# Channel attention on one core: fewer rows read twice, by a smaller accumulator and a stash in PSUM

## Chip, cores, metric

The kernel runs on one core of one Trainium2 chip. The metric is the device time of one execution in microseconds; medians are quoted. Engine names are those of the profile: PE (matmul), DVE (VectorE), ACT (ScalarE), SP (SyncE, which here only issues loads). A "row" below is one pixel of 96 bf16 channels in each of the 128 partitions: 192 bytes per partition, 24.6 KB in all.

## The reference

```python
H = W = 384; C = 96; r = 24                 # x: (1, 384, 384, 96) bf16, w1: (96, 24), w2: (24, 96)
gap = jnp.mean(xf, 1); gmp = jnp.amax(xf, 1)  # over all 147456 pixels
h_a = relu(gap @ w1);  h_m = relu(gmp @ w1)
scale = sigmoid(h_a @ w2 + h_m @ w2)          # one factor per channel
return x * scale[:, None, None, :]
```

The output needs a factor that depends on all of x. So x is read once for the mean and the maximum, kept on the chip as far as it fits, and then multiplied and stored. Each partition has 1152 rows, 221,184 bytes, which is more than its part of the on-chip memory (SBUF) can hold beside the other tiles.

## The kernel before

Phase 1 loads x in chunks of 64 rows. DVE folds each chunk into `acc`, 64 rows of running maxima; PE adds the rows up with a column of ones. The cache holds NCR = 1028 rows; U = 124 rows don't fit. Those are loaded first, into places that later chunks overwrite, and must be read a second time in phase 2.

```python
ACC_ROWS = 64; FIRST_P2_CHUNKS = (16, 32); TAIL_P1_CHUNK = 16; LAG = 6; PA_SLOT = 1
...
    NCR = min(NPP, budget // ROWB)      # rows in the cache
    U = NPP - NCR                       # rows that are read twice
...
    # phase 1, for each chunk
        nc.sync.dma_start(out=xt, in_=xv[:, r0 : r0 + n, :])
        ...
                nc.vector.tensor_tensor(out=acc[:, 0:m, :], in0=acc[:, 0:m, :],
                                        in1=xt[:, a : a + m, :], op=ALU.max)
        ...
    # then a tree over the 64 rows of acc, transpose, two small matmuls, sigmoid -> scale
    # phase 2: rows of the U are loaded into acc (64 rows), srow (8 rows) and,
    # once its first contents are stored, a place in the cache (52 rows)
            nc.sync.dma_start(out=ap, in_=xv[:, r : r + n, :])
    ...
    for ci, (r0, n) in enumerate(chunks2):
        mult(ap, n)          # DVE: cache rows *= scale
        store(r0, n, ap)     # DMA issued by ACT
        ...
                nc.sync.dma_start(out=u["ap"], in_=xv[:, u["r0"] : u["r0"] + u["n"], :])
        while loaded and loaded[0][0] + LAG <= ci:
            _, u = loaded.pop(0)
            mult(u["ap"], u["n"])
            store(u["r0"], u["n"], u["ap"])
```

## Time and profile before

| | before |
|---|---|
| median time | 159.76 us (159.47 to 159.88) |
| span of the profile | 157.7 us |
| HBM read / written | 31.37 MB / 28.31 MB |
| phase 1, DMA rate 8 to 66 us | 426 GB/s |
| last DVE maximum done / column maxima (`pmax`) done / `scale` ready | 74.5 / 78.8 / 80.8 us |
| stores, DMA rate 100 to 140 us | 430 GB/s |

The two rows of the page below cut the span into 40 slices of 3.94 us: the busy share of the 16 DMA engines in tenths, and what they moved.

```profile
DMA  5999999999999999950179999999999999999995
GB/s 184 407 437 433 424 433 421 419 436 418 433 415 440 415 427 419 425 208 0 50 259 399 390 399 287 374 436 420 430 433 423 428 436 433 424 440 421 427 436 212
```

DMA is full in phase 1 and again in phase 2; between them, in slices 18 and 19 (the first is slice 0), it has little or nothing to do. From the last load packet of phase 1 (its end is at 70.7 us) to the first store (issued at 81.85 us) it is 11 us; this stretch is called the bubble below. (The Trainium skill, "HBM Reference", section "Specifications (TRN2)", says that a core streaming alone gets about 425 GB/s; this trace agrees with 426 and 430.)

The next view groups instructions by line and shape: busy time in all, mean ns of one, then the idle time in front of them and what ended it.

```profile
L169 DVE TENSOR_TENSOR acc<-acc,cache 128x6144 bf16<-128x6144 bf16 x14 | 47.0, 3358 | 6.6 <-DMA cache<-in_x_dram 6.6
L232 DVE TENSOR_TENSOR cache<-cache,scale 128x6144 bf16<-128x6144 bf16 x15 | 49.3, 3348 | 0.0
L192 DVE TENSOR_TENSOR acc<-acc 128x3072 bf16<-128x3072 bf16 x1 | 1.8, 1759 | 0.0
```

A 64-row maximum takes 3.36 us and its chunk comes every 3.69 us, so DVE waits for DMA. A 64-row multiply takes 3.35 us; the DMA needs 1.573 MB / 430 GB/s = 3.66 us to store it. DMA is the limit in both phases, and DVE is close behind.

The chain of waits (start us, us, what) around the bubble:

```profile
70.30 3.17 DVE acc L169
73.49 0.97 DVE acc L169
74.48 1.77 DVE acc L192
...
78.55 0.22 DVE pmax_sb L201
...
80.58 0.26 ACT scale L229
```

The last chunks' maxima are done at 74.46 us, and a tree of six steps, of which the first takes 1.77 us, ends at 78.77 us. Then come the small steps to `scale`.

Stretches of phase 2 (window, length, busy us of each engine, PE clock, busy share of DMA, GB/s):

```profile
core 0: us, PE busy (x) PEld busy (x) DVE busy (x) ACT busy (x) POOL busy (x), PEclk, DMA share, GB/s
94.00:100.00 6.00, 0.00 (x0) 0.00 (x0) 6.00 (x2) 0.00 (x0) 0.00 (x0) 0.50 1.00 291
100.00:140.00 40.00, 0.00 (x0) 0.00 (x0) 39.99 (x14) 0.00 (x0) 0.00 (x0) 0.50 1.01 430
88.00:157.00 69.00, 0.00 (x0) 0.00 (x0) 51.99 (x17) 0.00 (x0) 0.00 (x0) 0.50 0.99 409
```

One thing stands out: from 94 to 100 us the DMA engines are as busy as ever (share 1.00), but move 291 GB/s. The 52-row re-read into the cache was issued at 92.4 us.

### The profile page before, as it was taken

The numbers are of one execution on the slowest core, as the hardware profiler recorded it, in microseconds if no ns is written. First come the engines' busy times: TensorE is split into PE (matmuls) and PEld (weight loads), VectorE is DVE, ScalarE is ACT, GpSimd is POOL, SyncE is SP. The second block draws the span as 40 slices with busy tenths as digits, with TensorE's granted clock in tenths as the row PEclk, the third lists the DMA queues.
The fourth block names the chain that finished last, engine by engine and source line by source line (L and its number), as shares of the span: only waits on it lengthen the run. The fifth ranks groups of instructions, "written<-read, shape, count | busy, mean of one in ns | idle before, by whom it ended". The sixth has DMA issues, their size and how long they took to land.

```text
span 157.7 us, 798 instructions
## 1 busy us (share of the span) xinstructions
PE 54.6 (35%) x299; PEld 26.2 (17%) x299; DVE 122.9 (78%) x51; ACT 2.5 (2%) x6; POOL 0.7 (0%) x6
## 2 busy tenths in 40 slices
PE   0299777739977777688010000000000000000000
PEld 0144333314433333334000000000000000000000
DVE  0258999959999999899969999999999999950000
ACT  3000000000000000001010000000000000000000
POOL 1000000000000000000000000000000000000000
PEclk9999999996999999999655555555555555555555
DMA  5999999999999999950179999999999999999995
GB/s 184 407 437 433 424 433 421 419 436 418 433 415 440 415 427 419 425 208 0 50 259 399 390 399 287 374 436 420 430 433 423 428 436 433 424 440 421 427 436 212
DMA packets 6343, 59.72 MB, mean 379 GB/s; under 512 B 836, under 2 KB 1092, under 8 KB 1604
## 3 DMA queue, kind: packets, MB, share of 16 engines
q1 hardware_dynamic: 3168, 31.36, 48.8%
q10 hardware_dynamic: 3172, 28.32, 42.9%
q8 instruction: 2, 0.03, 0.1%
q14 instruction: 1, 0.01, 0.0%
HBM read 31.37 MB, written 28.31 MB: 379 GB/s over the span
## 4 chain that ended last, share of the span: by engine, by line
DMA 44%; DVE 39%; issue 2%; DVEq 2%; PE 1%; ACT 0%; SPq 0%
DMA cache<-in_x_dram 44%; DVE cache L232 31%; DVE acc L169 3%; DVE acc L192 3%; DVE acc L232 2%; DVEq L331 2%; DVE srow_full L232 0%; SPq L133 0%; PE pmaxT_full L206 0%; DVE vt L207 0%; DVE hp L222 0%; PE misc_ps L228 0%; ACT scale L229 0%; DVE pmax_sb L201 0%; PE misc_ps L220 0%
## 5 line engine op out<-in xcount | busy, mean ns | idle before, releaser
L169 DVE TENSOR_TENSOR acc<-acc,cache 128x6144 bf16<-128x6144 bf16 (+3 forms) x18 | 57.2, 3180 | 8.6 <-DMA cache<-in_x_dram 8.4
L179 PE MATMUL misc_ps<-cache,ones_col 128*1 128x384 bf16 x288 | 53.0, 342 | 20.5 <-DMA cache<-in_x_dram 20.5
L232 DVE TENSOR_TENSOR cache<-cache,scale 128x6144 bf16<-128x6144 bf16 (+4 forms) x19 | 55.6, 2991 | 0.6 <-ACT scale L229 0.6
L179 PEld LDWEIGHTS <-ones_col 128*1 128x1 bf16 x288 | 25.1, 87 | 48.0 <-issue 27.3
L150 DVE COPY acc<-cache 128x6144 bf16<-128x6144 bf16 x1 | 1.8, 1760 | 6.0 <-DMA cache<-in_x_dram 6.0
L192 DVE TENSOR_TENSOR acc<-acc 128x3072 bf16<-128x3072 bf16 (+4 forms) x5 | 3.9, 779 | 0.2
L232 DVE TENSOR_TENSOR acc<-acc,scale 128x6144 bf16<-128x6144 bf16 x1 | 3.3, 3348 | 0.0
L206 PE MATMUL pmaxT_full<-ident,pmax_sb 128*96 128x128 bf16 x1 | 0.3, 339 | 3.9 <-DVE pmax_sb L201 3.9
L209 ACT ACTIVATE srow_full<-misc_ps 1x384 f32<-1x384 f32 x1 | 0.5, 481 | 70.9 <-PE misc_ps L179 70.9
L95 ACT ACT_TABLE_LOAD x1 | 1.3, 1283 | 1.2 <-PEq L320 1.2
L211 PE MATMUL misc_ps<-one,srow_full 1*96 1x1 f32 x8 | 0.8, 221 | 0.6 <-ACT srow_full L209 0.6
L211 PEld LDWEIGHTS misc_ps<-one,srow_full 1*96 1x96 f32 x8 | 0.7, 159 | 1.0 <-ACT srow_full L209 1.0
L206 PEld LDWEIGHTS <-pmax_sb 128*96 128x96 bf16 x1 | 0.2, 155 | 4.0 <-DVE pmax_sb L201 4.0
L94 DVE MEMSET warm<- 128x1 f32 x1 | 0.1, 59 | 0.8 <-PEq L320 0.8
L222 DVE TENSOR_TENSOR hp<-hrelu 24x128 bf16<-24x128 bf16 x1 | 0.3, 281 | 0.5 <-ACT hrelu L221 0.5
L207 DVE TENSOR_REDUCE vt<-pmaxT_full 96x1 bf16<-96x128 bf16 x1 | 0.3, 290 | 0.4 <-PE pmaxT_full L206 0.4
L232 DVE TENSOR_TENSOR srow_full<-srow_full,scale 128x768 bf16<-128x768 bf16 x1 | 0.5, 549 | 0.0
L228 PE MATMUL misc_ps<-w_sb,hp 24*128 24x96 bf16 x1 | 0.3, 258 | 0.6 <-DVE hp L222 0.6
L220 PE MATMUL misc_ps<-vt,w_sb 96*24 96x2 bf16 x1 | 0.2, 181 | 0.4 <-DVE vt L207 0.4
masks.py:199 POOL TENSOR_SCALAR_AFFINE_SELECT ident<-ident 128x128 bf16<-128x128 bf16 x1 | 0.3, 294 | 0.1
L229 ACT ACTIVATE scale<-misc_ps 128x96 bf16<-128x96 f32 x1 | 0.3, 251 | 0.7 <-PE misc_ps L228 0.7
L221 ACT ACTIVATE hrelu<-misc_ps 24x2 bf16<-24x2 f32 x1 | 0.2, 161 | 4.6 <-PE misc_ps L220 4.6
(12 smaller groups left out, 1.5 us busy)
## 6 DMA issues: line engine op xcount, KB each, us to landing
cache<-in_x_dram SPq DMA_DIRECT2D x15, 1536.0 KB, 27.1
out_dram<-cache ACTq DMA_DIRECT2D x15, 1536.0 KB, 14.0
cache<-in_x_dram SPq DMA_DIRECT2D x2, 1440.0 KB, 19.0
acc<-in_x_dram SPq DMA_DIRECT2D x1, 1536.0 KB, 6.4
out_dram<-acc ACTq DMA_DIRECT2D x1, 1536.0 KB, 6.5
cache<-in_x_dram SPq DMA_DIRECT2D x1, 1344.0 KB, 29.1
cache<-in_x_dram SPq DMA_DIRECT2D x1, 1248.0 KB, 10.2
out_dram<-cache ACTq DMA_DIRECT2D x1, 1248.0 KB, 13.5
```

Source lines behind the costliest of these rows:

```text
L95: nc.scalar.activation(out=warm2[:], in_=warm[:], func=ACT.Sigmoid)
L150: nc.vector.tensor_copy(out=acc[:, 0:m, :], in_=xt[:, 0:m, :])
L169: nc.vector.tensor_tensor(out=acc[:, 0:m, :], in0=acc[:, 0:m, :], in1=xt[:, a : a + m, :], op=ALU.max,)
L179: nc.tensor.matmul(sum_ps[:, 0 : g * C], ones_col[:], xt[:, g0 : g0 + g, :], start=(mm_i == 0), stop=(mm_i == total_mm - 1),)
L192: nc.vector.tensor_tensor(out=acc[:, 0:h, :], in0=acc[:, 0:h, :], in1=acc[:, h : 2 * h, :], op=ALU.max)
L206: nc.tensor.transpose(pmaxT_ps, pmax_sb[:], ident[:])
L207: nc.vector.reduce_max(out=vt[:, 1:2], in_=pmaxT_ps, axis=AX.X)
L209: nc.scalar.activation(out=srow[:, 0:MW], in_=sum_ps, func=ACT.Copy)
L211: nc.tensor.matmul(gap_ps, srow[:, g * C : (g + 1) * C], one11[:], start=(g == 0), stop=(g == G - 1),)
L222: nc.vector.tensor_tensor(out=hp[:], in0=hrelu[:, 0:1].to_broadcast([R, P]), in1=hrelu[:, 1:2].to_broadcast([R, P]), op=ALU.add,)
L232: nc.vector.tensor_tensor(out=xt_ap, in0=xt_ap, in1=scale[:].unsqueeze(1).to_broadcast([P, n, C]), op=ALU.mult,)
L331: with _tile.TileContext(nc) as tc:
```

## The change

Its intent is to read fewer rows twice. `acc` shrinks from 64 to 32 rows, and the cache grows by these 32. Another 32 of the remaining U = 92 rows are copied by ACT into PSUM, as fp32, while they pass through in phase 1, and DVE multiplies them out of PSUM later. 60 rows are read twice instead of 124. Loads and first stores are also put in another order. A "prefold" is in the diff but never does anything, since `acc_live` starts at its goal.

```diff
-ACC_ROWS = 64
-FIRST_P2_CHUNKS = (16, 32)
-TAIL_P1_CHUNK = 16
+ACC_ROWS = 32
+PREFOLD_TO = 32
+PS_ROWS = 32
+FIRST_P2_CHUNKS = (24, 32)
+STAGE_RELOAD_AFTER = 6
...
+    stash_rows = min(PS_ROWS, U, ps_rows_cap)
+        stash = psum.tile([P, stash_rows, C], FP32, tag="stash")
...
+    chunks1 += main_chunks[:k] + reload_chunks + main_chunks[k:] + tail_chunks
...
+            nc.scalar.activation(
+                out=stash[:, stashed : stashed + ns, :], in_=xt[:, 0:ns, :], func=ACT.Copy
+            )
...
-            m = min(ACC_ROWS, n - a)
+            m = min(acc_live, n - a)          # maxima in pieces of 32 rows
...
-    def mult(xt_ap, n):
+    def mult(out_ap, in_ap, n):
...
+            unc.append(dict(r0=sr0, n=sn, ap=cache[:, cr0 : cr0 + sn, :], after=ci,
+                            src=stash[:, sr0 - NCR : sr0 - NCR + sn, :]))
```

More of the change, by code (lines that the diff above doesn't have):

```diff
@@ L16 @@
 RB = 64
-ACC_ROWS = 64
-FIRST_P2_CHUNKS = (16, 32)
-TAIL_P1_CHUNK = 16
+ACC_ROWS = 32
+PREFOLD_TO = 32
+PREFOLD_CHUNKS_LEFT = 7
+PS_ROWS = 32
+FIRST_P2_CHUNKS = (24, 32)
+TAIL_PIECE = 16
+NTAIL = 2
 W_AFTER_CHUNK = 3
+STAGE_RELOAD_AFTER = 6
 LAG = 6
 PA_SLOT = 1
-NEG_BIG = -3.0e38
 SBUF_SAFETY = 256
@@ L51 @@
     G = max(1, min(RB, (BANK_F32 - 3 - C) // C))
-    MW = G * C
     const = ctx.enter_context(tc.tile_pool(name="const", bufs=1))
@@ L66 @@
     warm2 = small.tile([P, 1], FP32, tag="warm2")
-    srow_full = small.tile([P, MW], FP32, tag="srow")
-    srow = srow_full[0:1, :]
+    srow_full = small.tile([P, G * C], FP32, tag="srow")
     pmax_sb = small.tile([P, C], BF16, tag="pmax")
@@ L73 @@
     acc = small.tile([P, ACC_ROWS, C], BF16, tag="acc")
-    assert MW + 3 + C <= BANK_F32, f"{MW=} {C=} do not fit in one PSUM bank"
     misc_ps = psum.tile([P, BANK_F32], FP32, tag="misc_ps")
-    sum_ps = misc_ps[0:1, 0:MW]
-    gap_ps = misc_ps[0:C, MW : MW + 1]
-    h_ps = misc_ps[0:R, MW + 1 : MW + 3]
-    s_ps = misc_ps[:, MW + 3 : MW + 3 + C]
     pmaxT_full = psum.tile([P, nc.PSUM_BANK_SIZE_BYTES // 2], BF16, tag="pmaxT_ps")
     pmaxT_ps = pmaxT_full[0:C, 0:P]
+    ps_banks_left = nc.PSUM_NUM_BANKS - 2
+    ps_rows_cap = (ps_banks_left * nc.PSUM_BANK_SIZE_BYTES) // (C * 4)
     used = (const.current_size() + small.current_size()) // P
@@ L89 @@
     assert NCR >= max(2 * U, 1), f"{NCR=} {U=} {budget=}"
+    stash_rows = min(PS_ROWS, U, ps_rows_cap)
+    stash = None
+    if stash_rows > 0:
+        stash = psum.tile([P, stash_rows, C], FP32, tag="stash")
     cachep = ctx.enter_context(tc.tile_pool(name="cache", bufs=1))
@@ L98 @@
     masks.make_identity(nc, ident[:])
-    chunks1 = []
-    tail_rows = min(TAIL_P1_CHUNK, max(0, NCR - U))
+    SR0 = NCR - U
+    stage_chunks = []
     r = NCR
@@ L104 @@
         n = min(RB, NPP - r)
-        chunks1.append((r, n, r - U))
+        stage_chunks.append((r, n, r - U, "stage"))
         r += n
-    r = tail_rows
-    while r < NCR - U:
-        n = min(RB, NCR - U - r)
-        chunks1.append((r, n, r))
-        r += n
-    r = NCR - U
+    reload_chunks = []
+    r = SR0
     while r < NCR:
         n = min(RB, NCR - r)
-        chunks1.append((r, n, r))
+        reload_chunks.append((r, n, r, "reload"))
         r += n
-    if tail_rows > 0:
-        chunks1.append((0, tail_rows, 0))
-    assert sum(n for (_, n, _) in chunks1) == NPP
+    t0 = SR0 % RB if NPP >= RB else 0
+    ntail = NTAIL if t0 >= NTAIL * TAIL_PIECE else max(0, t0 // TAIL_PIECE)
+    tail_chunks = []
+    r = 0
+    rem = t0 - ntail * TAIL_PIECE
+    if rem > 0:
+        tail_chunks.append((0, rem, 0, "tail"))
+        r = rem
+    for _ in range(ntail):
+        tail_chunks.append((r, TAIL_PIECE, r, "tail"))
+        r += TAIL_PIECE
+    assert r == t0
+    main_chunks = []
+    r = t0
+    while r < SR0:
+        n = min(RB, SR0 - r)
+        main_chunks.append((r, n, r, "main"))
+        r += n
+    chunks1 = list(stage_chunks)
+    k = min(STAGE_RELOAD_AFTER, len(main_chunks))
+    chunks1 += main_chunks[:k] + reload_chunks + main_chunks[k:] + tail_chunks
+    assert sum(n for (_, n, _, _) in chunks1) == NPP
+    assert sorted((r0, n) for (r0, n, _, _) in chunks1) == sorted(
+        list((r0, n) for (r0, n, _, _) in stage_chunks + reload_chunks + tail_chunks + main_chunks)
+    )
     G = min(G, chunks1[0][1])
     MW = G * C
+    assert MW + 3 + C <= BANK_F32, f"{MW=} {C=} do not fit in one PSUM bank"
     sum_ps = misc_ps[0:1, 0:MW]
+    gap_ps = misc_ps[0:C, MW : MW + 1]
+    h_ps = misc_ps[0:R, MW + 1 : MW + 3]
+    s_ps = misc_ps[:, MW + 3 : MW + 3 + C]
+    srow = srow_full[0:1, 0:MW]
     def n_mm(nrows):
         return (nrows + G - 1) // G
-    total_mm = sum(n_mm(n) for (_, n, _) in chunks1)
+    total_mm = sum(n_mm(n) for (_, n, _, _) in chunks1)
+    full_idx = [i for i, c in enumerate(chunks1) if c[1] >= RB]
+    prefold_after = full_idx[-PREFOLD_CHUNKS_LEFT] if len(full_idx) > PREFOLD_CHUNKS_LEFT else -1
     mm_i = 0
     acc_valid = 0
-    for ci, (r0, n, h0) in enumerate(chunks1):
+    acc_live = PREFOLD_TO
+    stashed = 0
+    for ci, (r0, n, h0, kind) in enumerate(chunks1):
         xt = cache[:, h0 : h0 + n, :]
@@ L136 @@
             nc.scalar.dma_start(out=w2_sb[:], in_=w2)
+        if kind == "stage" and stash is not None and stashed < stash_rows and r0 == NCR + stashed:
+            ns = min(stash_rows - stashed, n)
+            nc.scalar.activation(
+                out=stash[:, stashed : stashed + ns, :], in_=xt[:, 0:ns, :], func=ACT.Copy
+            )
+            stashed += ns
         a = 0
         if acc_valid == 0:
-            if n >= 2 * ACC_ROWS:
+            if n >= 2 * acc_live:
                 nc.vector.tensor_tensor(
-                    out=acc[:, 0:ACC_ROWS, :],
-                    in0=xt[:, 0:ACC_ROWS, :],
-                    in1=xt[:, ACC_ROWS : 2 * ACC_ROWS, :],
+                    out=acc[:, 0:acc_live, :],
+                    in0=xt[:, 0:acc_live, :],
+                    in1=xt[:, acc_live : 2 * acc_live, :],
                     op=ALU.max,
                 )
-                acc_valid = ACC_ROWS
-                a = 2 * ACC_ROWS
+                acc_valid = acc_live
+                a = 2 * acc_live
             else:
-                m = min(ACC_ROWS, n)
+                m = min(acc_live, n)
                 nc.vector.tensor_copy(out=acc[:, 0:m, :], in_=xt[:, 0:m, :])
@@ L175 @@
             a += m
+        if ci == prefold_after:
+            while acc_live > PREFOLD_TO and acc_live % 2 == 0 and acc_valid == acc_live:
+                h = acc_live // 2
+                nc.vector.tensor_tensor(
+                    out=acc[:, 0:h, :], in0=acc[:, 0:h, :], in1=acc[:, h:acc_live, :], op=ALU.max
+                )
+                acc_live = h
+                acc_valid = h
         g0 = 0
@@ L187 @@
             g0 += g
+    assert stashed == stash_rows
     rr = acc_valid
@@ L207 @@
     nc.vector.reduce_max(out=vt[:, 1:2], in_=pmaxT_ps, axis=AX.X)
-    nc.scalar.activation(out=srow[:, 0:MW], in_=sum_ps, func=ACT.Copy)
+    nc.scalar.activation(out=srow, in_=sum_ps, func=ACT.Copy)
     for g in range(G):
@@ L229 @@
     nc.scalar.activation(out=scale[:], in_=s_ps, func=ACT.Sigmoid)
-    def mult(xt_ap, n):
+    def mult(out_ap, in_ap, n):
         nc.vector.tensor_tensor(
-            out=xt_ap,
-            in0=xt_ap,
+            out=out_ap,
+            in0=in_ap,
             in1=scale[:].unsqueeze(1).to_broadcast([P, n, C]),
@@ L252 @@
         r += n
+    unc_free = []
+    unc = []
+    r = NCR
+    stash_list = []
+    while r < NCR + stash_rows:
+        n = min(RB, NCR + stash_rows - r)
+        stash_list.append((r, n))
+        r += n
     free_regions = [
         (acc[:, :, :].rearrange("p r c -> p (r c)"), ACC_ROWS * C),
-        (srow_full[:, :].bitcast(BF16), 2 * MW),
+        (srow_full[:, :].bitcast(BF16), 2 * G * C),
     ]
-    unc_free = []
-    unc = []
-    if U > 0:
-        r = NCR
-        for fap, elems in free_regions:
-            n = min(elems // C, NPP - r)
-            if n <= 0:
-                break
-            ap = fap[:, 0 : n * C].rearrange("p (r c) -> p r c", c=C)
-            nc.sync.dma_start(out=ap, in_=xv[:, r : r + n, :])
-            unc_free.append((r, n, ap))
-            r += n
-        ci = 0
-        while r < NPP:
-            while ci < len(chunks2) and chunks2[ci][1] < min(RB, NPP - r):
-                ci += 1
-            assert ci < len(chunks2)
-            cr0, cn = chunks2[ci]
-            n = min(cn, NPP - r)
-            unc.append(dict(r0=r, n=n, ap=cache[:, cr0 : cr0 + n, :], after=ci))
-            r += n
-            ci += 1
+    for fap, elems in free_regions:
+        n = min(elems // C, NPP - r)
+        if n <= 0:
+            continue
+        ap = fap[:, 0 : n * C].rearrange("p (r c) -> p r c", c=C)
+        nc.sync.dma_start(out=ap, in_=xv[:, r : r + n, :])
+        unc_free.append((r, n, ap))
+        r += n
+    ci = 0
+    pos = 0
+    while stash_list or r < NPP:
+        want = min(RB, NPP - r) if r < NPP else stash_list[0][1]
+        while ci < len(chunks2) and chunks2[ci][1] < want:
+            ci += 1
+        assert ci < len(chunks2), "no cached chunk region large enough"
+        cr0, cn = chunks2[ci]
+        if r >= NPP:
+            sr0, sn = stash_list.pop(0)
+            unc.append(dict(r0=sr0, n=sn, ap=cache[:, cr0 : cr0 + sn, :], after=ci,
+                            src=stash[:, sr0 - NCR : sr0 - NCR + sn, :]))
+        else:
+            n = min(cn, NPP - r)
+            unc.append(dict(r0=r, n=n, ap=cache[:, cr0 : cr0 + n, :], after=ci, src=None))
+            r += n
+        ci += 1
     loaded = []
@@ L284 @@
         ap = cache[:, r0 : r0 + n, :]
-        mult(ap, n)
+        mult(ap, ap, n)
         store(r0, n, ap)
@@ L288 @@
             for (ur0, un, uap) in unc_free:
-                mult(uap, un)
+                mult(uap, uap, un)
                 store(ur0, un, uap)
@@ L293 @@
             if u["after"] == ci:
-                nc.sync.dma_start(out=u["ap"], in_=xv[:, u["r0"] : u["r0"] + u["n"], :])
+                if u["src"] is None:
+                    nc.sync.dma_start(out=u["ap"], in_=xv[:, u["r0"] : u["r0"] + u["n"], :])
                 loaded.append((ci, u))
@@ L297 @@
             _, u = loaded.pop(0)
-            mult(u["ap"], u["n"])
+            mult(u["ap"], u["src"] if u["src"] is not None else u["ap"], u["n"])
             store(u["r0"], u["n"], u["ap"])
     for (ur0, un, uap) in unc_free:
-        mult(uap, un)
+        mult(uap, uap, un)
         store(ur0, un, uap)
     for (_, u) in loaded:
-        mult(u["ap"], u["n"])
+        mult(u["ap"], u["src"] if u["src"] is not None else u["ap"], u["n"])
         store(u["r0"], u["n"], u["ap"])
```

## The prediction

> **What bounds it now.** The page shows two phases of DMA traffic around a bubble. Phase 1 loads x once: slices 2 to 17 move 425 GB/s, and in the DVE timeline 64-row chunks are consumed every 3.69 us while one maximum takes 3.36 us, so DVE idles 0.33 us per chunk "<-DMA". Phase 1 is DMA bound and its last 60-row chunk lands at 70.2 us. Bubble: the chain of waits shows DVE 3.17 + 0.97 us on the last chunks, a 64-row tree of about 4.3 us to pmax at 78.77, then 2.06 us of small steps; scale is ready at 80.83. Phase 2 multiplies and stores; DVE needs 3.27 us per 64 rows and is done at 140 us, but DMA runs at 430 GB/s until 156. DMA bound again. It moves 1152 rows per partition of stores plus re-reads of 124 rows (31.37 MB read against 28.31 MB of x: 3.05 MB), of which 116 rows come after 78.8 us.
>
> **What the change does.**
> 1. Re-reads drop from 124 to 60 rows: acc shrinks by 32 rows, so the cache holds 32 more; 32 rows are kept in PSUM as fp32. That is 64 x 24.6 KB = 1.57 MB less, 3.7 us at 430 GB/s, all in DMA-bound phase 2.
> 2. The tree starts from 32 rows: its first step (1.76 us) is gone.
> 3. The maximum is done in 32-row pieces: by the 128x3072 forms 1.76 us each plus 0.03 us gap, 3.58 us per 64 rows instead of 3.38. Still under 3.69, margin 0.11 us per chunk. The last chunks are now 64 and 8 rows: about 70.7 + 3.58 + 0.59 = 74.9 against 74.46 before. With the shorter tree pmax is due near 77.4, scale near 79.4: 1.4 us earlier.
> 4. The first multiply has 24 rows, not 16 (est. 1.36 against 0.96 us), so the first store leaves near 80.9, 1.0 us earlier than now (81.85). Only 20 rows instead of 52 are re-read into the cache, into the first chunk's place, so in an early DMA gap rather than at 92.4 us. In the trace the 94 to 100 us stretch of that re-read ran near 290 GB/s (about 2 us lost); I expect that dip to shrink.
> 5. Added: one ScalarE copy of 128x3072 into PSUM. By the Trainium skill, "ScalarE: Activation LUTs", section "What ACT_TABLE_LOAD costs", 186 ns + 0.833 ns per element: est. 2.75 us, hidden near 7 to 10 us on an idle engine. One multiply reads PSUM fp32; by the Trainium skill, "VectorE: DVE Perf Modes", "The perf-mode tier table", such a tensor_tensor has only 1x: est. 3.35 us for 32 rows instead of 1.75. DVE is by then some 50 rows ahead of the stores, so it costs nothing. The prefold code is never active.
>
> **Sum.** DVE feeds DMA without gaps from about 88 us in both kernels. From there before moves about 1148 rows, after about 1056: 5.3 us less; saturation starts perhaps 0.9 us later because more rows come before the first 64-row chunk; the smaller dip gives back up to 1 us. Gain 4.4 to 5.5 us.
>
> **Predicted: 154.7 us, 8 in 10 between 152.8 and 156.8.** Faster by over 2%: 0.86; within 2%: 0.13; slower: 0.01.
>
> **Right if:** HBM read falls to 29.8 MB; pmax ends near 77.4 us; DVE still idles on DMA in phase 1; the stash multiply is near 3.35 us with no DMA dip after it; DMA ends near 151 us.
>
> **Wrong if:** the 0.11 us margin isn't enough and DVE becomes phase 1's limit (pmax then no earlier); or the early stores leave DMA idle near 82 to 88 us, wasting the removed re-reads; or writes alone run slower than the mix.

## The result

The changed kernel took 154.00 us (153.83 to 154.25, 8 runs), the kernel before 159.71 us (159.43 to 160.07, 15 runs). The ratio is 0.9641, with a 95 % interval of 0.9632 to 0.9651.

The page's DMA rows after the change (slices of 3.81 us):

```profile
DMA  5999999999999999991057999999999999999995
GB/s 165 409 442 423 439 420 429 429 401 439 426 426 426 426 426 421 423 411 67 2 149 292 298 436 436 426 429 433 423 421 441 426 436 426 429 429 433 423 422 218
```

The chain of waits around the bubble, to be read against the one above:

```profile
70.82 1.77 DVE acc L207
72.61 1.77 DVE acc L207
74.41 0.57 DVE acc L207
75.00 0.97 DVE acc L239
...
77.27 0.22 DVE pmax_sb L248
...
79.29 0.26 ACT scale L276
```

The last 64 rows are now folded in two pieces. They and the 8 rows behind them end at 74.98 us, half a microsecond later than before; the tree is shorter by its 1.77 us step, `pmax` is done at 77.49 us instead of 78.77, and `scale` at 79.55 instead of 80.84.

The groups by shape that answer to those of before, and the two that are new:

```profile
L207 DVE TENSOR_TENSOR acc<-acc,cache 128x3072 bf16<-128x3072 bf16 x32 | 56.3, 1758 | 6.0 <-DMA cache<-in_x_dram 4.0
L279 DVE TENSOR_TENSOR cache<-cache,scale 128x6144 bf16<-128x6144 bf16 x15 | 49.3, 3348 | 0.0
L279 DVE TENSOR_TENSOR cache<-stash,scale 128x3072 bf16<-128x3072 f32 x1 | 3.3, 3347 | 0.0
L171 ACT ACTIVATE stash<-cache 128x3072 f32<-128x3072 bf16 x1 | 2.7, 2735 | 4.5 <-DMA cache<-in_x_dram 4.5
```

Two pieces of 1.76 us and two gaps of some 0.03 us are 3.58 us per 64 rows; DVE is still just faster than DMA in phase 1. The multiply out of PSUM took 3.35 us, and the copy 2.73 us on an idle engine. Both agree with the skill's figures that the prediction used.

The same stretches of phase 2:

```profile
94.00:100.00 6.00, 0.00 (x0) 0.00 (x0) 6.00 (x3) 0.00 (x0) 0.00 (x0) 0.50 1.01 430
100.00:140.00 40.00, 0.00 (x0) 0.00 (x0) 40.00 (x14) 0.00 (x0) 0.00 (x0) 0.50 1.01 429
88.00:157.00 69.00, 0.00 (x0) 0.00 (x0) 52.37 (x18) 0.00 (x0) 0.00 (x0) 0.52 0.91 388
```

The dip at 94 to 100 us is gone; the steady rate is unchanged. A shorter dip now stands where the 20-row re-read runs, in slice 22 of the page (83.8 to 87.6 us): DMA is full and moves 298 GB/s. HBM reads are 29.80 MB. With the window from 88 us on, the gain can be added up. Before, 69 us x 409 GB/s = 28.2 MB were still to be moved at 88 us; after, 69 x 388 = 26.8 MB. That is 1.45 MB less, 3.4 us at 430 GB/s. The dip cost 6 us x (430 - 291) GB/s = 0.83 MB, 1.9 us. Together they make 5.3 us, and the last data packet of the trace ends at 151.0 us instead of 156.3.

### The profile page after: what moved, and what is told of

Its sections match the earlier page's. It is cut to its first block, busy times and chain, and to the rows that moved or that the text cites. A ratio compares the mean times of both kernels' runs of the same rounds, so it can differ in the third digit from the quotient of the medians.

```text
span 152.3 us, 823 instructions
## 1 busy us (share of the span) xinstructions
PE 55.0 (36%) x299; PEld 26.4 (17%) x299; DVE 125.5 (82%) x68; ACT 5.3 (3%) x7; POOL 0.7 (0%) x6
## 3 DMA queue, kind: packets, MB, share of 16 engines
HBM read 29.80 MB, written 28.31 MB: 382 GB/s over the span
## 4 chain that ended last, share of the span: by engine, by line
DMA 41%; DVE 40%; PE 5%; issue 2%; DVEq 2%; ACT 0%; SPq 0%
DMA cache<-in_x_dram 41%; DVE cache L279 34%; PE misc_ps L225 4%; DVE acc L207 3%; DVEq L390 2%; DVE acc L239 1%; DVE acc L279 1%; DVE srow_full L279 0%; PE pmaxT_full L253 0%; SPq L165 0%; DVE vt L254 0%; DVE hp L269 0%; PE misc_ps L275 0%; ACT scale L276 0%; DVE pmax_sb L248 0%
## 5 line engine op out<-in xcount | busy, mean ns | idle before, releaser
L207 DVE TENSOR_TENSOR acc<-acc,cache 128x3072 bf16<-128x3072 bf16 (+2 forms) x35 | 59.9, 1712 | 6.1 <-DMA cache<-in_x_dram 4.0
L178 DVE TENSOR_TENSOR acc<-cache 128x3072 bf16<-128x3072 bf16 x1 | 1.8, 1759 | 6.3 <-DMA cache<-in_x_dram 6.3
L279 DVE TENSOR_TENSOR cache<-stash,scale 128x3072 bf16<-128x3072 f32 x1 | 3.3, 3347 | 0.0
L171 ACT ACTIVATE stash<-cache 128x3072 f32<-128x3072 bf16 x1 | 2.7, 2735 | 4.5 <-DMA cache<-in_x_dram 4.5
L239 DVE TENSOR_TENSOR acc<-acc 128x1536 bf16<-128x1536 bf16 (+3 forms) x4 | 2.1, 533 | 0.1
L279 DVE TENSOR_TENSOR acc<-acc,scale 128x3072 bf16<-128x3072 bf16 x1 | 1.8, 1750 | 0.0
```

What stands on the lines that cost most here:

```text
L171: nc.scalar.activation(out=stash[:, stashed : stashed + ns, :], in_=xt[:, 0:ns, :], func=ACT.Copy)
L178: nc.vector.tensor_tensor(out=acc[:, 0:acc_live, :], in0=xt[:, 0:acc_live, :], in1=xt[:, acc_live : 2 * acc_live, :], op=ALU.max,)
L239: nc.vector.tensor_tensor(out=acc[:, 0:h, :], in0=acc[:, 0:h, :], in1=acc[:, h : 2 * h, :], op=ALU.max)
L279: nc.vector.tensor_tensor(out=out_ap, in0=in_ap, in1=scale[:].unsqueeze(1).to_broadcast([P, n, C]), op=ALU.mult,)
```

## Experiments

The theory was that the gain is the removed re-reads plus the shorter tree, and that the re-read amid the stores costs more than its bytes. Rivals: the new order of loads and stores brings it (layout), or the shorter bubble alone does (bubble). All runs gave correct results except the one that says otherwise. Runs of one block shared a chip and the runs of the kernel before, whose median was 159.52 to 159.60 us.

### The parts one by one

The changed kernel with one or both of its parts undone:

```diff
 order_only:  -ACC_ROWS = 32   +ACC_ROWS = 64
              -PREFOLD_TO = 32 +PREFOLD_TO = 64
              -PS_ROWS = 32    +PS_ROWS = 0
 psum_only:   -ACC_ROWS = 32   +ACC_ROWS = 64
              -PREFOLD_TO = 32 +PREFOLD_TO = 64
 acc_only:    -PS_ROWS = 32    +PS_ROWS = 0
```

> The changed kernel with 64-row maxima and no PSUM rows: only the new order of the loads and the 24-row first store are left; 124 rows are re-read, as before. Re-read theory (the gain is the removed re-reads plus the shorter tree): no gain, 160.0 us (159.3 to 160.6), since the first store leaves some 0.5 us later. Rival, layout theory (the new order of loads and stores brings much of the 5.7 us): 157 us or less.

> As order_only, but with the 32 PSUM rows: the cache re-read shrinks from 52 to 20 rows, the tree stays that of 64 rows. Re-read theory: 32 rows x 24.6 KB at 430 GB/s = 1.83 us less than order_only, plus up to 1 us from the smaller dip of the DMA rate: 157.0 to 158.2 us. Bubble theory (the gain is the shorter tree): within 0.5 us of order_only. The multiply from PSUM near 3.35 us in both.

> The changed kernel without the PSUM rows: maxima in 32-row pieces, shorter tree, 32 rows more in the cache; 92 rows re-read, 52 of them into the cache amid the stores. Re-read theory: about 156.5 to 157.5 us, so that acc_only and psum_only each bring roughly half. Bubble theory: near 154.5 us, almost the whole gain. pmax should end near 77.4 us.

| run | rows read twice: acc, srow, cache | median us | ratio to before (95 %) |
|---|---|---|---|
| order_only | 64, 8, 52 | 159.85 | 1.0013 (0.9999 to 1.0028) |
| psum_only | 64, 8, 20 | 157.06 | 0.9818 (0.9784 to 0.9853) |
| acc_only | 32, 8, 52 | 157.75 | 0.9883 (0.9868 to 0.9898) |
| changed | 32, 8, 20 | 154.00 | 0.9641 (0.9632 to 0.9651) |

The new order alone brings nothing: the layout theory falls. The smaller `acc` without the PSUM rows (the shorter tree and 32 rows fewer read twice) brings 2.1 us against order_only, not nearly all: the bubble theory falls too. Of these 2.1 us the bytes of the 32 rows are 1.8 us; the 0.3 us left for the shorter tree are within the noise. The PSUM rows alone bring 2.8 us, as expected. But acc_only came out worse than expected (157.75 against 156.5 to 157.5), and by the medians the two parts together bring 5.85 us, 0.96 us more than their sum. Do they help each other? The windows from 100 us to the end show what DMA still had to move, in this order: kernel before, acc_only, psum_only, changed kernel. The last line is the end of psum_only.

```profile
100.00:157.00 57.00, 0.00 (x0) 0.00 (x0) 39.99 (x14) 0.00 (x0) 0.00 (x0) 0.50 0.99 420
100.00:157.00 57.00, 0.00 (x0) 0.00 (x0) 38.71 (x13) 0.00 (x0) 0.00 (x0) 0.50 0.96 406
100.00:157.00 57.00, 0.00 (x0) 0.00 (x0) 41.76 (x15) 0.00 (x0) 0.00 (x0) 0.50 0.93 392
100.00:157.00 57.00, 0.00 (x0) 0.00 (x0) 40.37 (x14) 0.00 (x0) 0.00 (x0) 0.52 0.89 379
152.40:154.60 2.20, 0.00 (x0) 0.00 (x0) 0.00 (x0) 0.00 (x0) 0.00 (x0) 0.50 0.11 43
```

Times 57 us, these are 23.9, 23.1, 22.3 and 21.6 MB. Against the kernel before, acc_only has 0.8 MB less to move, psum_only 1.6 and the changed kernel 2.3: the sum of the two, within the rounding. At 430 GB/s that is 1.9, 3.7 and 5.4 us. By the medians against the kernel before, acc_only gained 1.8 us and the changed kernel 5.7, but psum_only only 2.5. The profiled run of psum_only (157.66 us) lost the rest at its very end, where DMA moved 43 GB/s for 2 us. In the last 2 us of its stores it moved the bytes of 4 rows, the other fast traces here 24 to 33. The fast runs of psum_only scatter from 155.94 to 157.66 us, more than those of any other kernel, and the two fastest are 3.6 us under the kernel before, as the bytes say. So nothing here shows that the parts help each other: what DMA has left adds up, and the 0.96 us is as large as the scatter of psum_only. Only one of its runs has a trace; that the other slower ones lost their time in the same way isn't shown.

Two stretches of acc_only (columns as in the windows above) suggest why it brought no more than its bytes:

```profile
core 0: us, PE busy (x) PEld busy (x) DVE busy (x) ACT busy (x) POOL busy (x), PEclk, DMA share, GB/s
86.00:90.00 4.00, 0.00 (x0) 0.00 (x0) 4.00 (x2) 0.00 (x0) 0.00 (x0) 0.50 0.80 323
94.00:100.00 6.00, 0.00 (x0) 0.00 (x0) 6.00 (x3) 0.00 (x0) 0.00 (x0) 0.50 1.04 318
```

The dip of the 52-row re-read is still there (318 GB/s), and there is a new loss at 86 to 90 us, with DMA busy for 0.80 of the time. `scale` comes earlier, but the first 64-row store is not issued before 88.0 us, and the smaller `acc` leaves fewer rows to store until then. In the changed kernel the 20-row re-read was issued at 83.85 us. It does not simply fill that gap; the first line is the changed kernel, the second acc_only, which reads nothing there:

```profile
84.00:88.00 4.00, 0.00 (x0) 0.00 (x0) 4.00 (x4) 0.00 (x0) 0.00 (x0) 0.50 1.00 308
84.00:88.00 4.00, 0.00 (x0) 0.00 (x0) 4.00 (x4) 0.00 (x0) 0.00 (x0) 0.50 0.97 387
```

With the re-read, DMA is busy all the time but moves less. From 84 to 94 us the changed kernel moved 3.83 MB (383 GB/s), of which 0.49 MB are the 20 rows, and acc_only 3.71 MB (371 GB/s). So acc_only stored 0.37 MB more: the early re-read cost most of its own bytes.

One run was left aside. One of the five executions of order_only took 218 us, with matmuls of 688 ns on average (345 ns in the changed kernel), and the profile fell into that one; its profile isn't used.

### What the re-read amid the stores costs

```diff
 no_reread (kernel before):
-                nc.sync.dma_start(out=u["ap"], in_=xv[:, u["r0"] : u["r0"] + u["n"], :])
                 loaded.append((ci, u))
 late_reread (kernel before):
-        ci = 0
+        ci = 9          # first place in the cache that is tried for the re-read
         while r < NPP:
```

> The kernel before without its 52-row re-read into the cache; the rows are multiplied from stale data and the result is wrong on purpose. If the re-read costs its bytes only: 1.28 MB at 430 GB/s = 3.0 us, so 156.8 us. If the dip of the DMA rate at 94 to 100 us belongs to this re-read, another 2 us or so: 154.5 to 155.3 us, and no dip there. If the dip belongs to the start of the stores, it stays in the trace.

> The kernel before, its 52-row re-read put into the region of a later chunk: issued near 125 us instead of 92 us, and multiplied last. If the dip of the DMA rate belongs to the re-read wherever it stands among stores, the dip moves with it, 94 to 100 us runs near 430 GB/s, and the time stays: 159.2 to 160.2 us. If it belongs to the ramp at the start of the stores, the time falls by 1 us or more (158.5 us or less).

no_reread took 155.24 us (ratio 0.9725, 0.9711 to 0.9739). That is 4.3 us less than before, where the bytes account for 3.0. Its output is wrong, which doesn't matter for the time. late_reread took 158.91 us (ratio 0.9960, 0.9946 to 0.9974), between the ranges of the two theories. Its re-read was issued at 122.2 us. The windows of no_reread over the stretch of the dip and the steady stretch behind it:

```profile
94.00:100.00 6.00, 0.00 (x0) 0.00 (x0) 6.00 (x2) 0.00 (x0) 0.00 (x0) 0.50 0.99 413
100.00:140.00 40.00, 0.00 (x0) 0.00 (x0) 39.83 (x14) 0.00 (x0) 0.00 (x0) 0.50 1.01 425
```

The windows of late_reread at the old and at the new place of the re-read:

```profile
94.00:100.00 6.00, 0.00 (x0) 0.00 (x0) 6.00 (x2) 0.00 (x0) 0.00 (x0) 0.50 1.01 424
124.00:128.00 4.00, 0.00 (x0) 0.00 (x0) 4.00 (x2) 0.00 (x0) 0.00 (x0) 0.50 0.99 323
```

Without the re-read there is no dip, and when the re-read moves, the dip moves with it. So the dip belongs to the re-read, not to the ramp of the stores. It is not a fixed sum: late_reread loses 4 us x (430 - 323) = 0.43 MB, 1.0 us, about half, and is 0.6 us faster. In the packets of the kernel before, 12,288-byte stores that normally take 460 ns have a median of 792 ns at 94 to 96 us, just before the re-read's own packets begin to move. Why the queues lose time when a read starts among stores, these runs don't say; nor do they separate whether the re-read of the changed kernel loses less because it is smaller or because it comes earlier. no_reread also falls short of the full sum, 3.0 + 1.9 us, since its stores run at 425 GB/s from 100 to 140 us and not at 430. All six kernels without a re-read amid the stores ran at 421 to 425 GB/s in that stretch, and those whose re-read lay before it at 427 to 430; the cause is open.

### Is the margin of phase 1 real?

The prediction's main worry was that 32-row pieces leave DVE only 0.11 us per chunk.

```diff
 pieces16 (changed kernel):
-ACC_ROWS = 32
-PREFOLD_TO = 32
+ACC_ROWS = 16
+PREFOLD_TO = 16
```

> The changed kernel with maxima in 16-row pieces: 16 rows fewer re-read, one tree step fewer. If the margin of phase 1 is the sum of the pieces' durations (4 x (0.96 + 0.03) = 3.95 us per 64 rows against 3.69 us of DMA), DVE becomes the limit: pmax 2 to 4 us later than in the changed kernel (79.5 to 81.5 us) and the time 156 to 158 us. If DVE only waits for DMA there and the piece size doesn't matter: 153.0 to 153.8 us.

It took 156.19 us (ratio 0.9788, 0.9775 to 0.9802), 2.2 us more than the changed kernel although it reads 16 rows fewer twice. The DVE timeline (start us, us, engine, line, ...) shows twenty pieces and no wait:

```profile
59.10 19.43 DVE L207 TENSOR_TENSOR acc<-acc,cache 128x1536 bf16<-128x1536 bf16 x20
78.57 1.25 DVE L239 TENSOR_TENSOR acc<-acc 128x768 bf16<-128x768 bf16 x3
79.85 0.21 DVE L248 TENSOR_TENSOR pmax_sb<-acc 128x96 bf16<-128x96 bf16 x1
```

`pmax` was done at 80.06 us, 2.6 us later than with 32-row pieces. 64 rows cost 4 x 0.97 us here (19.43 us / 20), more than the DMA's 3.69. The margin is the sum of the pieces' durations, and 32 rows is the last halving of `acc` that pays.

### Nothing read twice amid the stores

By the kernel's own formula (`ps_rows_cap`), PSUM has room for twice as many rows if pairs of bf16 are kept in its 32-bit words. DVE copies them as 32-bit integers, and the multiply reads them through a bf16 view. 52 rows are enough to do without a re-read into the cache.

```diff
 packed (changed kernel):
-PS_ROWS = 32
+PS_ROWS = 52
-    ps_rows_cap = (...) // (C * 4)
+    ps_rows_cap = (...) // (C * 2)
-        stash = psum.tile([P, stash_rows, C], FP32, tag="stash")
+        stash32 = psum.tile([P, stash_rows * C // 2], INT32, tag="stash")
+        stash = stash32[:, :].bitcast(BF16).rearrange("p (r c) -> p r c", c=C)
-            nc.scalar.activation(out=stash[...], in_=xt[:, 0:ns, :], func=ACT.Copy)
+            nc.vector.tensor_single_scalar(out=stash32[...], in_=xt[...].bitcast(INT32),
+                                           scalar=0, op=ALU.bitwise_or)
 packed_tail (packed):
-FIRST_P2_CHUNKS = (24, 32)
-PA_SLOT = 1
+FIRST_P2_CHUNKS = (16, 16, 32, 32)
+PA_SLOT = 2
+    # the last 64-row load in pieces of 32, 16 and 16 rows
```

> The changed kernel with the PSUM rows kept as pairs of bf16 (52 rows instead of 32, copied by DVE as 32-bit words), so that nothing is re-read into the cache. Re-read theory: 20 rows = 1.15 us and their dip are gone, but that re-read stood partly in a DMA gap near 86 us, so 152.5 to 153.3 us. DVE pays some 2.75 us for the copy near 7 us, of which 2.0 us is its idle time there; pmax at most 0.3 us later. The multiply of 52 rows out of PSUM: 2.75 us if bf16 from PSUM runs as from SBUF, 5.4 us if it runs at one element per cycle; either way no gap of the stores.

> As packed, with the last 64-row load cut into 32, 16 and 16 rows and the first stores 16, 16, 32, 32 rows. If what is left is the wait from the last landing to the first store and the gap of the stores at 86 to 90 us: scale ready about 1.5 us earlier (near 78 us), DMA busy without gap from the first store, 150.0 to 151.8 us. If the bubble is hidden by something else, no gain over packed.

packed took 153.29 us (ratio 0.9610, 0.9597 to 0.9623), at the upper end of what was expected. Groups by shape in packed:

```profile
L173 DVE TENSOR_SCALAR stash<-cache 128x2496 int32<-128x2496 int32 x1 | 2.8, 2760 | 6.1 <-DMA cache<-in_x_dram 6.1
L284 DVE TENSOR_TENSOR cache<-stash,scale 128x4992 bf16<-128x4992 bf16 x1 | 2.7, 2747 | 0.0
```

The multiply of 52 rows out of PSUM took 2.75 us, as long as the same shape from SBUF in the kernel before (2748 ns). But without the re-read the gap is back:

```profile
86.00:90.00 4.00, 0.00 (x0) 0.00 (x0) 4.00 (x2) 0.00 (x0) 0.00 (x0) 0.50 0.73 296
92.00:108.00 16.00, 0.00 (x0) 0.00 (x0) 16.00 (x6) 0.00 (x0) 0.00 (x0) 0.50 1.00 419
```

DMA is busy for 0.73 of 86 to 90 us. packed gained 0.7 us on the changed kernel, where the bytes of 20 rows are 1.1 us. The re-read in the gap was not free for that: at 94 us the changed kernel had 24.2 MB left (384 GB/s over the 63 us to 157 us) and packed 23.6 MB (375 GB/s), a difference of 23 rows (the `scale` of packed came 0.3 us earlier, too). But from 100 to 140 us the stores of packed ran at 424 GB/s and those of the changed kernel at 429, which takes 0.5 us back.

packed_tail took 153.40 us (ratio 0.9611, 0.9598 to 0.9624) and missed its expectation by 1.6 us. `pmax` came at 77.6 us, no earlier than in packed. The DVE timeline shows the reason:

```profile
67.14 7.92 DVE L216 TENSOR_TENSOR acc<-acc,cache 128x3072 bf16<-128x3072 bf16 x6 [0.16 <-DMA cache<-in_x_dram]
75.09 2.24 DVE L248 TENSOR_TENSOR acc<-acc 128x1536 bf16<-128x1536 bf16 x4
```

From 67.1 us, when the last whole 64-row load landed, DVE worked through six pieces without a break until 75.06 us. It can start a chunk only when all of it has landed, and is only 0.11 us per chunk faster than DMA, so it ends about one 64-row chunk behind. Smaller pieces at the very end can't change that. The smaller first stores did close the gap at 86 to 90 us (409 GB/s), but another opened at 90 to 92 us (246 GB/s).

### Smaller transfers

```diff
 loads32  (packed):  every load of phase 1 in 32 rows
+LB = 32
-STAGE_RELOAD_AFTER = 6
+STAGE_RELOAD_AFTER = 12
-        n = min(RB, ...)      +        n = min(LB, ...)     # stage, reload and main chunks
 stores32 (packed):
-FIRST_P2_CHUNKS = (24, 32)
+FIRST_P2_CHUNKS = (16, 16) + (32,) * 12
 both32: both;  changed_again: the changed kernel
```

> The changed kernel itself, on the same chip as the three that follow: 153.8 to 154.3 us.

> packed with every load of phase 1 in 32 rows instead of 64. Lag theory, formed from packed_tail (there DVE ran without a break from the landing of the last 64-row load at 67.1 us, so that small last pieces changed nothing: DVE is only 0.11 us per 64 rows faster than DMA and cannot work off a whole load's lag): loads of 32 rows halve the lag, pmax some 1.8 us earlier (near 75.4 us), time 151.3 to 152.0 us. If the lag isn't the cause, pmax stays near 77.1 us and the time near 153.3 us.

> packed with first stores of 16, 16 and twelve times 32 rows, instead of 24, 32 and then 64. Ramp theory: the DMA gap at 86 to 90 us (298 and 295 GB/s in packed) is the wait for the first 64-row multiply; stores of 32 rows keep DMA fed, the gap goes (over 400 GB/s from 84 us on), 151.9 to 152.6 us. If the gap has another cause it stays and the time is 153.3 us.

> loads32 and stores32 together: 149.8 to 151.2 us if the two gains add.

| run | median us | ratio to before (95 %) |
|---|---|---|
| changed_again | 154.03 | 0.9652 (0.9638 to 0.9665) |
| loads32 | 152.91 | 0.9580 (0.9564 to 0.9596) |
| stores32 | 153.48 | 0.9615 (0.9602 to 0.9629) |
| both32 | 152.96 | 0.9566 (0.9544 to 0.9588) |

All three missed: loads32 by 0.9 us, stores32 by 0.9 us, both32 by 1.8 us. The windows show phase 1 of loads32, then the start of the stores in stores32:

```profile
8.00:66.00 58.00, 44.88 (x246) 20.53 (x245) 54.58 (x32) 0.00 (x0) 0.00 (x0) 1.00 1.02 417
```

```profile
86.00:90.00 4.00, 0.00 (x0) 0.00 (x0) 4.00 (x3) 0.00 (x0) 0.00 (x0) 0.50 1.00 409
92.00:108.00 16.00, 0.00 (x0) 0.00 (x0) 16.00 (x9) 0.00 (x0) 0.00 (x0) 0.50 1.01 414
```

In stores32 the gap at 86 to 90 us did close (409 GB/s against 296), yet the time did not fall. The steady rate of the 32-row stores was 414 GB/s where packed had 419. At 94 us stores32 had 0.25 MB less to move than packed (371 against 375 GB/s over the 63 us to 157 us), which is 0.6 us; from 100 to 140 us it lost half of that again (421 against 424 GB/s); and its last packet ended at 150.2 us against 150.0, after 24 rows in the last 2 us where packed moved 33. In loads32 `pmax` came 0.6 us earlier than in packed, not 1.8: phase 1 ran at 417 GB/s instead of 426, which makes its 28.3 MB some 1.4 us longer by these rates; in the trace the last load packet ended at 71.7 us instead of 70.6. DVE ended 2.5 us after that packet (74.2 us), where it was 4.2 us in packed (74.8 us), so the lag did shrink by 1.7 us. In the traces a packet of 6,144 bytes (32 rows of a partition) takes 236 ns, one of 12,288 bytes 462 ns: two small ones are 2 % dearer than a large one. That is what the shorter lag was paid with. Of these kernels loads32 and both32 are the fastest, 0.7 to 0.9 % under the changed kernel by their ratios; the difference between the two is within the noise.

## Why the prediction was right

The time (154.0 against 154.7 us) and the direction were right. Point by point:

- **DMA bounds both phases, and the removed re-reads pay.** Right. Without the two parts the new order brings nothing (order_only), and the steady rate of the stores is the same before and after (430 and 429 GB/s).
- **Bubble.** Right in its times, though not in what they were worth (see the sum): `pmax` 77.49 us (77.4 predicted), `scale` 79.55 (79.4), first store issued at 80.97 (80.9), end of the last maxima 74.98 (74.9).
- **Added work is hidden.** Right: 2.73 and 3.35 us (2.75 and 3.35 predicted), and DMA ran at 429 GB/s from 100 to 140 us across the PSUM multiply at 105 us.
- **Margin of phase 1.** Right, and pieces16 shows what happens beyond it.
- **The sum.** Its total was near, but two terms were mis-sized. The prediction said 92 rows less to move after 88 us (5.3 us), minus 0.9 us for a later start of full DMA, plus up to 1 us for the smaller dip. Only 64 of the 92 are rows no longer read twice; the other 28 were to be moved before 88 us because the stores start earlier. The bytes left at 88 us before were as said (28.2 MB / 24.6 KB = 1148 rows); after, they were 1089 rows and not 1056, so 59 rows or 3.4 us, where the prediction had 4.4 us net. So the earlier start moved nothing more. The other term is the dip: it cost 1.9 us in the trace and is gone from 94 to 100 us whole (the shorter one of the 20-row re-read lies before 88 us, within the 3.4 us). Two errors of about 1 us nearly cancelled, so that the total came this near is partly luck.
- **The risk it named.** Under "wrong if" the prediction has early stores that leave DMA idle near 82 to 88 us. Part of this happened. `scale` came 1.3 us earlier, but from 72 to 94 us the changed kernel moved 5.6 MB and the kernel before 5.7 MB (150 and 141 GB/s up to 84 us, then 383 and 401 GB/s).

## What to carry to other kernels

Where DMA is the limit, count the bytes that are moved while it is full: rows removed there were worth their time here, while 1.3 us cut from the bubble brought next to nothing, it seems because too few rows were ready to store (acc_only). The 52-row read that started among stores cost 1 to 2 us more than its bytes. To judge whether two parts of a change help each other, compare what is left to move and not the medians alone, when one of them scatters. DVE, which takes in whole chunks and is barely faster than DMA, ended a full chunk behind; smaller chunks shorten that lag, but here the halved packets cost 2 % of the load rate. Add up the durations of the pieces before a buffer is halved: 32-row pieces fit under the DMA's 3.69 us per 64 rows, 16-row pieces did not.

## What the Trainium skill lacked or had wrong

- "VectorE: DVE Perf Modes", section "The perf-mode tier table": it gives `tensor_tensor` with any operand in PSUM the 1x mode. With bf16 read from PSUM the multiply of 128x4992 took 2.75 us, the same as from SBUF (2748 ns), which is 0.55 ns per element of a partition. With fp32 in PSUM it was half as fast (128x3072 in 3347 ns, 1.09 ns). The same page's section "Why PSUM operands drop a tier" allows the faster mode, so the table should say it by type.
- "DMA: Bandwidth & Descriptors", section "Measured (HBM→SBUF, 128 partitions, SWDGE, issued from GpSimd)": the page has single trn2 rates for loads issued from SP, but no comparison of rates by bytes per partition for transfers issued from SP or ACT. Here 12,288 bytes per partition ran at 426 GB/s and 6,144 at 417 (packets of 462 and 236 ns).
- No page: a re-read that starts among stores lowers the rate of busy DMA engines, to 291 GB/s over 6 us (1.9 us lost) in one place and to 323 GB/s over 4 us (1.0 us) in another with 52 rows, and to 308 GB/s over 4 us with 20 rows.
- No page: from 100 to 140 us the stores ran at 421 to 425 GB/s in the six kernels without a re-read among them, and at 427 to 430 GB/s where one lay before. late_reread shows both: 423 GB/s from 94 to 120 us, before its re-read, and 432 from 134 to 154 us, behind it. Not explained here.
